# Weight loads on another queue and a sum two steps later, in a kernel of attention and two feed-forward layers

## The chip, the core and the metric

The kernel runs on one core of a Trainium2 chip. A core has five engines, each with its own instruction stream in a fixed order: TensorE (PE; its weight loads are shown as PEld), VectorE (DVE), ScalarE (ACT), GpSimd (POOL) and SyncE (SP), which here only asks for transfers. They wait for each other through semaphores. Transfers run on 16 DMA engines; an engine that asks for one spends time in its own stream on the request. The metric is device time in microseconds (us) of one execution, the median of several runs.

## The reference

Three stages follow each other; everything is float32 (weights of the two layers come as 64-bit floats).

```python
q_bits = (einsum('bhsd,dk->bhsk', q, proj) > 0)      # 6 bits each; k the same
mask = q_bucket[:, :, :, None] == k_bucket[:, :, None, :]
scores = where(mask, scale * q @ k.T, -1e9)
attn = exp(scores - max(scores)); attn = attn / (sum(attn) + 1e-9)
x = attn @ v                                         # 2 batches, 8 heads, 768 rows, 64 columns
x = ((1 / (1 + exp(-(x @ w_gate)))) * (x @ w_val)) @ w_out     # 1536 tokens, 512 -> 1536 -> 512
h = x @ w_in; y = (h * cos(h)) @ w_out2                        # 512 -> 2048 -> 512
```

## The kernel before

**The attention** goes over 96 steps g: 16 heads times 6 blocks of 128 query rows, with a tail of nine more steps. In each step a table of names (`ORDER`) says in which order parts of several blocks are issued; the order of instructions on each engine is the order in which the code issues them. For block g: `scores` (PE, two steps ahead), `rowmax` (DVE, L412), `expo` (ACT, L419: the exponential, one per step, so its starts mark the steps), `norm` (POOL, L454: scales a block's row by its sum, three steps later). Three blocks form a group u; a head has two. The three norms of a group are issued in three consecutive steps, all after `coef` of that group (DVE). Once they are done PE transposes the group, two column blocks a step (`ptrans`, L470), ACT and DVE split the result in a high and a low part (`phi` L475, `plo` L480), and PE multiplies with the values (`pv`, L490 and L491).

Every value tile holds a high and a low half, so the product `o` of a head has two halves of 64 partitions that must be added. `fin_act` (ACT, L499) copies `o` into `e`. At the end of a head pair, every 12 steps, it asks SP for two transfers that line up the halves, `ef<-e` (L507) and `e<-e` (L508). `fin_sum` (POOL, L513) then adds them, `fin_hi` (ACT, L529) and `fin_lo` (POOL, L533) split the sum into the layers' input `xy`. The call of step g puts these three into steps g + `SUM_AT`, g + `HIGH_AT` and g + `LOW_AT`, as the last piece (`PREP`) of the step. I call the step in which `fin_act` ends a pair the pair's end: 19, 31, 43, 55, 67, 79, 91 and 103.

Beside this run the inputs of later heads (`trans`: PE transposes, ACT evacuates into `xf` at L303, POOL splits into `x` at L304 and L307, SP distributes it at L348; `values`: POOL, L269 and L272, tile `vs`) and the first weights of the layers. `early_weights` (piece `W` of each step, behind the exponential) loads a weight block of 512 KB as 64-bit words into one of three `raw` tiles (`load_raw`, L133 and L139) at steps 14, 18 and 22, and from step 26 on converts one block in three steps, every ten steps, six in all (`convert_parts`: ACT `wp` L148, DVE L150, L154, L164). After the third part the tile is free and the next load is asked for.

**The layers** follow (`moe`): products on PE (L694, L756, L783), the rest of the weights loaded and converted on the way.

Of the kernel before, what the change touches and what calls it, by code (L numbers as in the profile page):

```python
# [18 lines left out]
P = 128  # L19
# [8 lines left out]
BITS_AT = (-10, -7)  # L28
VALUES_AT = (-3, -1)

SUM_AT, HIGH_AT, LOW_AT = 1, 5, 5
BIG = float(2.0**34)
CUT = float(2.0**30)
INV2PI = 1.0 / (2.0 * math.pi)
# [5 lines left out]
def lsh_attention_glu_moe_cos_moe(  # L40
# [13 lines left out]
    nc = tc.nc  # L54
# [16 lines left out]
    NEARLY = 6  # L71
# [9 lines left out]
    def constants():  # L81
        srow = xy[NC - 1].bitcast(F32)[0:1, 0, 0, 0 : 2 * D].rearrange("p (d two) -> p d two", two=2)
        make_identity(nc, ident)
        nc.vector.memset(pw.bitcast(F32), 0.0)
        nc.vector.memset(qscale[0:D], -SCALE)
        nc.vector.memset(qscale[D:P], 1.0)
        nc.vector.memset(halfpi, math.pi / 2)
        nc.vector.memset(quarter, 0.25)


        nc.vector.memset(srow, 0.0)
        k0, half = D // 2, BIG / 2
        for part, value, lo, hi in (
            (0, 1.0, 0, 3 * NB),
            (1, -1.0, 2 * NB, 3 * NB),
            (0, -BIG, k0, k0 + NB),
            (0, half, k0 + NB, k0 + 3 * NB),
            (1, -1.0, k0 + NB, k0 + 2 * NB),
        ):
            nc.vector.memset(srow[:, lo:hi, part : part + 1], value)  # L100
# [24 lines left out]

    raws = {}

    def load_raw(key):
        nm, f, _ = key
        rw = wraw.tile([P, 512], I64, tag="raw", name=f"raw_{nm}{f}")  # L130
        if nm in ("g", "v", "i"):
            src = {"g": w_gate, "v": w_val, "i": w_in2}[nm]
            nc.sync.dma_start(  # L133
                rw.rearrange("p (k c) -> p k c", k=KT),
                src[:, f * P : (f + 1) * P].rearrange("(k p) c -> p k c", p=P),
            )
        else:
            src = {"o": w_out1, "z": w_out2}[nm]
            nc.sync.dma_start(rw, src[f * P : (f + 1) * P, :])  # L139
        raws[key] = rw  # L140

    def convert_parts(key):
# [63 lines left out]
    def lead(key):  # L206
        nm, f, again = key
        if again:
            return 4, 2
        return {"g": (8, 4), "v": (7, 3), "i": (6, 3), "o": (5, 2), "z": (4, 3)}[nm]  # L210

    order = sorted(use, key=lambda kk: use[kk] - lead(kk)[0])
    done = 0
# [7 lines left out]

    loaded = 0

    def load_to(n):
        nonlocal loaded
        while loaded < min(n, len(order)):
            load_raw(order[loaded])
            loaded += 1


    def attention():
        nonlocal done
        parts = None
        with ExitStack() as st:
# [14 lines left out]
            def load(hd, nm, t0=0, t1=T, eng=nc.sync):  # L249
                b, h = divmod(hd, H)  # L250
                if nm == "v":
                    raw[hd, "v"] = nat.tile([P, 2, T * D], F32, tag="nv", name=f"nv{hd}", bufs=1)
                    nc.sync.dma_start(
                        raw[hd, "v"], v[b, h : h + 2].rearrange("h (p t) d -> p h (t d)", p=P)
                    )
                    return
                if hd not in raw:
                    raw[hd] = nat.tile([P, T, 2 * D], F32, tag="nqk", name=f"nqk{hd}")
                i = "qk".index(nm)
                eng.dma_start(  # L260
                    raw[hd][:, t0:t1, i * D : (i + 1) * D],
                    (q, k)[i][b, h].rearrange("(p t) d -> p t d", p=P)[:, t0:t1, :],
                )
# [274 lines left out]
            WL, WC = (14, 18, 22), 26  # L538
# [32 lines left out]
            def run_todo(step):  # L571
                for fn in todo.pop(step, []):
                    e = fn()
                    if e is not None:
                        late.append(e)

            with tc.manual_schedule(
                engines={
                    mybir.EngineType.PE,
                    mybir.EngineType.Activation,  # L580
                    mybir.EngineType.DVE,
                    mybir.EngineType.Pool,
                    mybir.EngineType.SP,
                }
            ):
                for t0 in (0, 3):
                    load(0, "q", t0, t0 + 3)
                    load(0, "k", t0, t0 + 3, eng=nc.scalar)
                constants()
                for g in range(2):  # L590
                    nc.sync.dma_start(pj[D * g : D * g + D, :], proj)
                nc.sync.dma_start(
                    bcode, xy[NC - 1].bitcast(F32)[0:1, 0, 0, 0 : 2 * D].rearrange("p (d two) -> p d two", two=2)
                )
                load(1, "q")
                load(1, "k")
                load(0, "v")
                load(2, "k")
                load(2, "q")
                bit_weights()  # L600
                evac = [trans(0, half, fast=True) for half in range(2)]
                for fn in evac:
                    fn()
                evac = [bits(0, half) for half in range(2)]
                evac += [trans(1, half, fast=True) for half in range(2)]
                for fn in evac:
                    fn()
                values(0)
                values(1)
                run_todo(-2)  # L610
                run_todo(-1)
                scores(0)
                scores(1)
                rowmax(0)
                late.extend(bits(1, half) for half in range(2))
                for g in range(NG + LAG + 2):
                    wa, wb = 2 * (g - LAG), 2 * (g - LAG) + 1
                    fin = (wb - 2) // T if 0 <= wb - 2 < NW and (wb - 2) % T == T - 1 else None

                    def finish_group():  # L620
                        fin_act(fin)
                        if fin % 4 == 3:
                            at(g + SUM_AT, lambda u=fin: fin_sum(u))
                            at(g + HIGH_AT, lambda u=fin: fin_hi(u))
                            at(g + LOW_AT, lambda u=fin: fin_lo(u))

                    def early_weights():
                        nonlocal done, parts
                        if g in WL:
                            load_to(1 + WL.index(g))  # L630
                        if done < NEARLY and g >= WC and (g - WC) % WSTEP == 0:
                            parts = convert_parts(order[done])
                        if parts is not None and next(parts, parts) is parts:
                            parts = None
                            done += 1
                            load_to(done + 3)

                    live_a, live_b, live_g = 0 <= wa < NW, 0 <= wb < NW, g < NG
                    third = 0 < g <= NG and g % 3 == 0
                    ops = {  # L640
                        "PVb": (0 <= wb - 2 < NW, lambda: pv(wb - 2)),
                        "FIN": (fin is not None, finish_group),
                        "Tb": (live_b, lambda: ptrans(wb)),
                        "LOa": (live_a, lambda: plo(wa)),
                        "EXP": (live_g, lambda: expo(g)),
                        "PVa": (live_a and fin is None, lambda: pv(wa)),
                        "MIN": (g + 1 < NG, lambda: rowmax(g + 1)),
                        "HIb": (live_b, lambda: phi(wb)),
                        "Ta": (0 <= wa + 2 < NW, lambda: ptrans(wa + 2)),
                        "COEF": (third, lambda: coef(g // 3 - 1)),  # L650
                        "LOb": (live_b, lambda: plo(wb)),
                        "NRM": (0 <= g - 3 < NG, lambda: norm(g - 3)),
                        "LATE": (True, run_late),
                        "W": (True, early_weights),
                        "S": (g + 2 < NG, lambda: scores(g + 2)),
                        "PVaF": (live_a and fin is not None, lambda: pv(wa)),
                        "PREP": (True, lambda: run_todo(g)),
                        "HIa": (0 <= wa + 2 < NW, lambda: phi(wa + 2)),
                    }
                    for name in ORDER if g >= LAG - 1 else FILL:  # L660
                        on, fn = ops[name]
                        if on:
                            fn()
                for step in sorted(todo):
                    run_todo(step)
# [209 lines left out]
```

## Time and profile before

| | us |
|---|---|
| median of 3 runs | 837.98 |
| lowest, highest | 836.65, 838.01 |
| the profiled execution: its time | 835.46 |
| the profiled execution: its span, first to last instruction | 833.7 |
| busy in the span: PE, DVE, ACT, POOL | 803.9, 601.4, 464.2, 327.1 |

The rows below come from the profiled execution. Times count from the start of its span; 1.76 us of its own time lie outside the span. Idle time of an engine is put down to the last releaser that the profile sees.

### The profile page before, as it was taken

What the parts mean: (1) busy time and instruction counts of PE and PEld (TensorE: products, weight loads), DVE (VectorE), ACT (ScalarE), POOL (GpSimd) and SP (SyncE); (2) the same over time, 40 slices, a digit from 0 to 9 for tenths busy, and PEclk for the clock granted to TensorE, in tenths of its full rate; (3) what the DMA queues carried; (4) which work ended last, traced back from release to release, by engine and by line L of the source; (5) the groups of instructions that cost most, each with busy time, mean ns of one, the idle gap of its engine ahead of it and who ended that gap; (6) DMA issues with size and microseconds to landing.
All of it is one profiled execution on the core that took longest, in us unless ns stands there. A gap on an engine that the chain in (4) does not pass through costs nothing.

```text
span 833.7 us, 11798 instructions
## 1 busy us (share of the span) xinstructions
PE 803.9 (96%) x3984; PEld 678.4 (81%) x3984; DVE 601.4 (72%) x996; ACT 464.2 (56%) x896; POOL 327.1 (39%) x315
## 2 busy tenths in 40 slices
PE   6998999999988999999999999999999999999998
PEld 4888788978877888888888888888788888868886
DVE  7998989989988444555554248787777777787773
ACT  5887788888877322233223234456666666664442
POOL 4858788787776211122112112230322222222221
PEclk9999999999999999999999999999999999999999
DMA  7775766576531223222232112341333323333222
GB/s 161 181 193 134 183 160 156 144 179 166 133 74 29 70 77 102 76 76 76 75 91 91 47 51 76 102 127 50 109 96 99 97 84 99 101 104 133 95 74 101
DMA packets 69068, 89.05 MB, mean 107 GB/s; under 512 B 29520, under 2 KB 52048, under 8 KB 69008
## 3 DMA queue, kind: packets, MB, share of 16 engines
q1 hardware_dynamic: 68208, 88.10, 37.7%
q8 instruction: 31, 0.51, 0.3%
q10 hardware_dynamic: 800, 0.20, 0.1%
q14 instruction: 29, 0.24, 0.1%
HBM read 59.77 MB, written 3.15 MB: 75 GB/s over the span
## 4 chain that ended last, share of the span: by engine, by line
PE 78%; POOL 5%; DMA 4%; issue 4%; ACT 4%; DVE 4%; SPq 1%; ACTq 0%; POOLq 0%; DVEq 0%
PE a L783 15%; PE ph L694 13%; PE pv L694 12%; PE a L756 12%; PE pg L694 12%; PE t L470 4%; POOL p L454 2%; PE s L401 2%; PE s L404 2%; PE o L491 2%; PE o L490 2%; DMA ef<-e 2%; ACT p L419 1%; DMA e<-e 1%; POOL ef L513 1%
## 5 line engine op out<-in xcount | busy, mean ns | idle before, releaser
L694 PE MATMUL ph<-xy,ih 128*128 128x512 f32 x384 | 118.2, 389 | 0.0
L480 DVE TENSOR_TENSOR pl<-t,ph 128x384 fp32r<-128x384 f32 x192 | 102.8, 549 | 20.8 <-ACT ph L475 18.7
L120 ACT CAST gh<-g 128x512 fp32r<-128x512 f32 x84 | 52.1, 620 | 112.4 <-PE a L783 44.8
L470 PE MATMUL t<-ident,p 128*128 128x128 f32 x576 | 99.6, 280 | 13.3 <-POOL p L454 10.0
L475 ACT CAST ph<-t 128x384 fp32r<-128x384 f32 x192 | 92.4, 484 | 31.4 <-PE t L470 26.1
L121 POOL TENSOR_TENSOR zl<-w_z,zh 128x512 fp32r<-128x512 f32 x32 | 41.9, 1310 | 169.8 <-ACT zh L120 169.8
L454 POOL TENSOR_SCALAR p<-p,r,d 128x768 f32<-128x768 f32 x96 | 96.3, 1014 | 3.3 <-PE o L491 3.3
L470 PEld LDWEIGHTS t<-ident,p 128*128 128x128 f32 x576 | 73.7, 143 | 28.6 <-POOL p L454 13.0
L720 DVE TENSOR_TENSOR g<-pv,sg 128x512 f32<-128x512 f32 x36 | 24.8, 689 | 98.6 <-PE pv L694 98.6
L412 DVE TENSOR_REDUCE mn<-s 128x1 f32<-128x768 f32 x96 | 91.1, 949 | 1.0 <-PE s L404 0.8
L419 ACT ACTIVATE p<-s,mn 128x768 f32<-128x768 f32 x96 | 87.8, 914 | 3.9 <-DVE mn L412 3.6
L694 PE MATMUL pg<-xy,gh 128*128 128x512 f32 x288 | 89.4, 390 | 0.0
L694 PE MATMUL pv<-xy,vh 128*128 128x512 f32 x288 | 88.7, 389 | 0.0
L718 ACT ACTIVATE sg<-pg 128x512 f32<-128x512 f32 x36 | 21.4, 593 | 114.0 <-PE pg L694 114.0
L694 PEld LDWEIGHTS ph<-xy,ih 128*128 128x128 f32 x384 | 72.1, 188 | 14.9
L121 DVE TENSOR_TENSOR gl<-g,gh 128x512 fp32r<-128x512 f32 x84 | 59.7, 713 | 32.8 <-ACT gh L120 30.6
L490 PE MATMUL o<-ph,vs 128*128 128x384 f32 x192 | 79.9, 416 | 0.3 <-ACT e L499 0.3
L783 PE MATMUL a<-zh,gh 128*128 128x512 f32 x192 | 75.0, 391 | 1.1 <-ACT gh L120 0.4
L783 PE MATMUL a<-zl,gh 128*128 128x512 f32 x192 | 75.0, 390 | 0.7 <-POOL zl L121 0.7
L783 PE MATMUL a<-zh,gl 128*128 128x512 f32 x192 | 74.8, 390 | 0.0
L694 PE MATMUL ph<-xy,il 128*128 128x512 f32 x192 | 74.7, 389 | 0.0
L401 PE MATMUL s<-k,q 96*128 96x384 f32 x192 | 69.9, 364 | 4.4 <-ACT p L419 3.0
(107 smaller groups left out, 1835.4 us busy)
## 6 DMA issues: line engine op xcount, KB each, us to landing
raw_z<-in_moe_w_out SPq DMA_DIRECT2D x32, 512.0 KB, 3.3
raw_o<-in_moe_w_out SPq DMA_DIRECT2D x24, 512.0 KB, 3.3
q<-x SPq DMA_DIRECT2D x45, 192.0 KB, 3.1
k<-x SPq DMA_DIRECT2D x45, 192.0 KB, 3.4
raw_i<-in_moe_w_in SPq DMA_DIRECT2D x16, 512.0 KB, 3.8
raw_g<-in_moe_w_gate SPq DMA_DIRECT2D x12, 512.0 KB, 3.6
raw_v<-in_moe_w_val SPq DMA_DIRECT2D x12, 512.0 KB, 3.8
nv<-in_v SPq DMA_DIRECT2D x8, 384.0 KB, 4.5
```

The costliest lines, as they stand in the source:

```text
L121: sub.tensor_tensor(out=dst_l, in0=src, in1=dst_h.bitcast(F32), op=ALU.subtract)
L401: nc.tensor.matmul(o, hh["q2"][0:96, t, :], hh["k2"][0:96, sl, :], start=True, stop=False)
L412: nc.vector.tensor_reduce(mn_t[u][:, i : i + 1], s_t[g], axis=AX.XY, op=ALU.min)
L419: nc.scalar.activation(pt, s_t.pop(g), AF.Exp, bias=mn_t[u][:, i : i + 1], scale=-1.0, accum_out=sm_t[u][:, i : i + 1],)
L454: nc.gpsimd.tensor_scalar(out=pt, in0=pt, scalar1=r[:, i : i + 1], scalar2=d[:, i : i + 1], op0=ALU.mult, op1=ALU.add,)
L470: nc.tensor.transpose(pt[:, i, :], pv_[:, j * P : (j + 1) * P], ident)
L475: nc.scalar.copy(ph, pt_t[w])
L480: nc.vector.tensor_tensor(out=pl, in0=pt_t.pop(w), in1=ph_t[w].bitcast(F32), op=ALU.subtract)
L490: nc.tensor.matmul(o_t[u], vs[:, j, :], ph_t.pop(w), start=(j == 0), stop=False)
L694: nc.tensor.matmul(ps, w[:, kt, :], xy[c][:, hl, kt, :], start=(n == 0), stop=(n == 11))
L756: nc.tensor.matmul(acc[c, e], w[:, e, :], m, start=(f == 0 and n == 0), stop=(f == F1 - 1 and n == 2),)
L783: nc.tensor.matmul(acc[c, t], m[:, ts], w, start=(f == 0 and n == 0), stop=(f == F2 - 1 and n == 2),)
```

## The change

The weight loads that `early_weights` asks for go on ACT's queue and no longer on SP's. The load that follows a conversion is asked for in the step after the conversion's third part, not in the same step. `fin_sum` is issued three steps after a pair's end, not one. Loads in the layers stay on SP.

```diff
-SUM_AT, HIGH_AT, LOW_AT = 1, 5, 5
+SUM_AT, HIGH_AT, LOW_AT = 3, 5, 5
...
-    def load_raw(key):
+    def load_raw(key, eng):
...
-            nc.sync.dma_start(
+            eng.dma_start(
...
-            nc.sync.dma_start(rw, src[f * P : (f + 1) * P, :])
+            eng.dma_start(rw, src[f * P : (f + 1) * P, :])
...
-    def load_to(n):
+    def load_to(n, eng=nc.sync):
         nonlocal loaded
         while loaded < min(n, len(order)):
-            load_raw(order[loaded])
+            load_raw(order[loaded], eng)
             loaded += 1
...
                         if g in WL:
-                            load_to(1 + WL.index(g))
+                            load_to(1 + WL.index(g), nc.scalar)
                         if done < NEARLY and g >= WC and (g - WC) % WSTEP == 0:
                             parts = convert_parts(order[done])
                         if parts is not None and next(parts, parts) is parts:
                             parts = None
                             done += 1
-                            load_to(done + 3)
+                        elif parts is None and 0 < done <= NEARLY:
+                            load_to(done + 3, nc.scalar)
```

The instructions of PE and DVE stand in the same order as before. On POOL seven of the eight sums move (the last has nothing left to pass); here is the first, of the pair that ends at step 19, before:

```order
L454 TENSOR_SCALAR p_779<-p_779,r_827,d_828 128x768
L513 TENSOR_TENSOR ef_641<-e_519,ef_641 128x768
L304 TENSOR_SCALAR x_5_807<-xf_964 128x384
L307 TENSOR_TENSOR x_5_808<-xf_964,x_5_807 128x384
L454 TENSOR_SCALAR p_835<-p_835,r_948,d_949 128x768
L269 TENSOR_SCALAR vs_986<-nv_863 128x6x64
L272 TENSOR_TENSOR vs_986<-nv_863,vs_986 128x6x64
L454 TENSOR_SCALAR p_875<-p_875,r_948,d_949 128x768
L454 TENSOR_SCALAR p_909<-p_909,r_948,d_949 128x768
```

and with the change:

```order
L454 TENSOR_SCALAR p_779<-p_779,r_827,d_828 128x768
L304 TENSOR_SCALAR x_5_807<-xf_963 128x384
L307 TENSOR_TENSOR x_5_808<-xf_963,x_5_807 128x384
L454 TENSOR_SCALAR p_835<-p_835,r_947,d_948 128x768
L269 TENSOR_SCALAR vs_985<-nv_863 128x6x64
L272 TENSOR_TENSOR vs_985<-nv_863,vs_985 128x6x64
L454 TENSOR_SCALAR p_875<-p_875,r_947,d_948 128x768
L513 TENSOR_TENSOR ef_641<-e_519,ef_641 128x768
L454 TENSOR_SCALAR p_909<-p_909,r_947,d_948 128x768
```

The sum stood ahead of the split of `x`, the values and all three norms of the next group; now it stands behind all of these but the group's third norm.

ACT's stream gains nine requests. This is the one of step 29, after the first conversion; `p` is the exponential of the step, `ph` the high part of a transposed block. Before:

```order
L419 ACTIVATE p_1287,sm_1167<-s_1233,mn_1166 128x768
L475 CAST ph_1296<-t_1279 128x384
L475 CAST ph_1306<-t_1289 128x384
L419 ACTIVATE p_1343,sm_1294<-s_1264,mn_1293 128x768
L303 ACTIVATE xf_1353<-pt_1321,qscale 128x384
```

and with the change:

```order
L419 ACTIVATE p_1285,sm_1167<-s_1233,mn_1166 128x768
L133 DMA raw_v_1294<-in_moe_w_val 128x4x128
L475 CAST ph_1296<-t_1277 128x384
L475 CAST ph_1306<-t_1287 128x384
L419 ACTIVATE p_1343,sm_1292<-s_1262,mn_1291 128x768
L303 ACTIVATE xf_1353<-pt_1321,qscale 128x384
```

The request stands between the exponential and the step's two high parts; in three of the nine steps the evacuation `xf` lies between the exponential and the request.

## Rows read from the trace of the kernel before

**Rows 1.** Windows: busy time per engine (instructions), granted TensorE clock, DMA share, GB/s.

```profile
25.00:60.00 35.00, 34.43 (x230) 31.63 (x229) 33.29 (x70) 29.92 (x68) 25.19 (x29) 1.00 0.76 189
60.00:75.00 15.00, 12.74 (x74) 11.31 (x73) 11.28 (x21) 10.80 (x25) 11.82 (x13) 0.89 0.71 164
...
72.00:74.00 2.00, 2.00 (x10) 1.81 (x8) 1.42 (x3) 1.98 (x6) 2.00 (x3) 0.50 1.05 284
...
300.00:570.00 270.00, 270.00 (x1193) 223.65 (x1192) 151.37 (x202) 92.31 (x164) 56.57 (x43) 1.00 0.26 82
```

**Rows 2.** Timeline of ACT, exponentials of steps 24, 27, 45, 48, 51, 54, 84, 87.

```profile
65.95 0.91 ACT L419 ACTIVATE p<-s,mn 128x768 f32<-128x768 f32 x1
...
77.33 0.91 ACT L419 ACTIVATE p<-s,mn 128x768 f32<-128x768 f32 x1
...
125.98 0.91 ACT L419 ACTIVATE p<-s,mn 128x768 f32<-128x768 f32 x1
...
133.63 0.91 ACT L419 ACTIVATE p<-s,mn 128x768 f32<-128x768 f32 x1
...
142.40 0.91 ACT L419 ACTIVATE p<-s,mn 128x768 f32<-128x768 f32 x1
...
149.80 0.91 ACT L419 ACTIVATE p<-s,mn 128x768 f32<-128x768 f32 x1
...
228.53 0.91 ACT L419 ACTIVATE p<-s,mn 128x768 f32<-128x768 f32 x1
...
238.99 0.91 ACT L419 ACTIVATE p<-s,mn 128x768 f32<-128x768 f32 x1
```

**Rows 3.** Timeline of POOL, first sum and what follows; the sixth sum.

```profile
62.93 1.83 POOL L513 TENSOR_TENSOR ef<-e,ef 128x768 f32<-128x768 f32 x1 [4.98 <-issue]
64.73 0.51 POOL L304 TENSOR_SCALAR x<-xf 128x384 fp32r<-128x384 f32 x1
...
66.33 0.99 POOL L454 TENSOR_SCALAR p<-p,r,d 128x768 f32<-128x768 f32 x1
67.28 0.52 POOL L269 TENSOR_SCALAR vs<-nv 128x384 fp32r<-128x384 f32 x1
...
68.86 1.95 POOL L454 TENSOR_SCALAR p<-p,r,d 128x768 f32<-128x768 f32 x2
...
225.63 1.85 POOL L513 TENSOR_TENSOR ef<-e,ef 128x768 f32<-128x768 f32 x1 [4.49 <-DMA e<-e]
```

**Rows 4.** Timeline of PE, transposes of a new group after sums one, three and six.

```profile
68.27 0.30 PE L470 MATMUL t<-ident,p 128*128 128x128 f32 x1
...
136.99 0.33 PE L470 MATMUL t<-ident,p 128*128 128x128 f32 x1 [0.58 <-POOL p L454]
...
230.22 0.27 PE L470 MATMUL t<-ident,p 128*128 128x128 f32 x1
```

**Rows 5.** Waits: engine, line, releaser, us in total, times, longest.

```profile
PE t L470 <- POOL p L454: 10.0, 11, 2.1
```

**Rows 6.** Timeline of ACT, evacuations xf, a conversion, the high part of a sum.

```profile
60.14 0.58 ACT L303 ACTIVATE xf<-pt,qscale 128x384 f32<-128x384 f32 x1 [0.60 <-PE pt L288]
...
130.12 0.67 ACT L148 ACTIVATE wp_g<-raw_g 128x512 f32<-128x512 f32 x1
...
137.73 0.93 ACT L529 CAST xy<-ef 128x512 fp32r<-128x512 f32 x2
...
222.73 0.58 ACT L303 ACTIVATE xf<-pt,qscale 128x384 f32<-128x384 f32 x1 [0.60 <-PE pt L288]
```

**Rows 7.** Source L513: shortest, median, longest of eight sums in ns.

```profile
L513 POOL TENSOR_TENSOR ef<-e,ef x8: 1829/1844/2509, 62.9 to 278.9; 128x768 f32<-128x768 f32 x8
```

**Rows 8.** Timeline of DVE beside the sum that starts at 159.97.

```profile
160.10 0.67 DVE L154 SCALAR_TENSOR_TENSOR wl_v<-wp_v,wl_v 128x512 int32<-128x512 int32 x1
```

**Rows 9.** Timelines of the queues: ACT's two requests, SP's longest in this stage.

```profile
0.73 1.06 ACTq L260 DMA_DIRECT2D nqk<-in_k  x2
...
149.41 1.49 SPq L260 DMA_DIRECT2D nqk<-in_k  x1
```

## The prediction, made before the changed kernel ran

> **What bounds the kernel now.** I read the windows first, to see which stage can give anything. In the layers PE has no gap: 270.00 of 270 us between 300 and 570 [rows 1]. Nothing in the change touches that stage, so what counts is when the attention ends, at about 275 us. In its undisturbed stretches PE is busy 34.43 of 35 us and DVE 33.29, ACT 29.92, so three engines are nearly full together; in the window 60 to 75 PE has 12.74 of 15 and all the others have dropped as well [rows 1]. Something holds them all there.
>
> Next the timeline of ACT, because its one exponential per step is a clock of the steps. Undisturbed, three steps take 149.80 − 142.40 = 7.40 us [rows 2]. The three steps 24 to 27 take 77.33 − 65.95 = 11.38, and steps 84 to 87 take 238.99 − 228.53 = 10.46 [rows 2]. I measured all 25 stretches of three steps between step 12 and step 87 in this way. Six are long, those that begin five steps after the end of a head pair (24, 36, 48, 60, 72, 84), with 11.38, 11.34, 8.77, 9.52, 8.87 and 10.46, together 60.34 us. Six undisturbed ones would be 44.40. The excess is **15.94 us**, and it is all that this change could return.
>
> Its origin is in POOL's timeline. The first sum (L513) starts at 62.93 after 4.98 us of idle POOL, waiting for the transfers that line up the halves; behind it stand x, the values and the three norms of the next group, of which the last two run as a pair from 68.86 [rows 3]. PE transposes the first of the three blocks at 68.27 and must wait for the other two [rows 4]; over the kernel it waits 10.0 us for norms in 11 places [rows 5]. The wait spreads to DVE and ACT, and in two of the six places the granted clock then falls to the lower of TensorE's levels, 1.2 GHz (0.50 between 72 and 74) [rows 1], right behind PE's wait.
>
> **The sum moved by two steps.** POOL reaches the first sum's old place at about 58 us and has to wait. Without the sum there, x starts when ACT's xf is done, 60.14 + 0.58, so at about 60.8 [rows 6]. From there the distances of the rows hold: 1.60 from x to the norm (64.73 to 66.33), 0.95 to the values, 1.58 to the second norm (67.28 to 68.86), 0.97 for it (half of 1.95) [rows 3]. That puts the sum at 65.9, three microseconds after it could start before. The sixth sum is the latest of its kind: it could start at 225.63 [rows 3], and its new place is 222.73 + 0.58 + 0.1 + 5.1 = 228.5 [rows 6]. So all six sums find their data there, with at least 2.9 us to spare, and POOL's wait is gone.
>
> What is late next is the group's third norm, since 1.84 us of sum [rows 7] now stand ahead of it. First pair: 65.9 + 1.84 + 0.99 = 68.7. PE would want this block a quarter of a microsecond behind the first, at 68.5 [rows 4], so it waits about 0.25. Sixth pair: 223.4 + 7.9 = 231.3 against 230.22 + 0.25 [rows 4], a wait of 0.86. The same sum for the four between gives 0 to 0.3. In total **1.7 us** of waiting stay.
>
> Two costs in the long stretches are not the sum's and stay too. First the high part of the sum: 0.93 us on ACT ahead of an exponential [rows 6]. In the stretch 48 to 51 (8.77, so 1.37 too long [rows 2]) PE waits only 0.58 for norms [rows 4]; the other 0.8 I put down to those casts. Taken five times, and 0.3 for the sixth, whose 3.06 are nearly all waits for norms (the longest, of 2.1 us [rows 5], is there), that is **4.3 us**. Second, conversions overlap the first two long stretches: an undisturbed stretch with one (45 to 48) takes 133.63 − 125.98 = 7.65, 0.25 more [rows 2], so **0.5**. Left over is what is removed: 15.94 − 1.7 − 4.3 − 0.5 = **9.4 us**. The seventh sum moves as well, but there POOL's norms wait for weight splits of the layers in any case; the eighth keeps its place. I count nothing for either.
>
> One rule speaks against the 1.84. The longest sum took 2.51 us [rows 7], and DVE's L154 started beside it, at 160.10 [rows 8]. The Trainium skill, SBUF — State Buffer, "Who interferes with whom", says that a DVE instruction with two SBUF inputs and a GpSimd instruction that reads SBUF exclude each other for a whole instruction; L154 is one, and this row agrees. By the rule, sums that land beside such an instruction in their new place would be the longer ones; by the median row they are not. It is the first rival below.
>
> **The requests on ACT.** Nine requests leave SP and enter ACT's stream. SP gains nothing that matters: behind them it stood waiting for POOL's x anyway. No conversion waits for these loads either, as each has at least 12 steps from its request, about 30 us. The raw tile has been free since DVE's L164 of the step before, so I see no wait at the request. The price is the request itself: two took 1.06 us at the start, 0.53 each [rows 9], so 4.8 us of ACT in all. How much reaches the path? The nearest row is a conversion's 0.67 us on ACT [rows 6], which together with its DVE parts lengthens a stretch by 0.25 [rows 2]. A request has no DVE part; I take 0.1 for each, **0.9 us**. What hides the rest is ACT's slack: it waits 0.60 for PE ahead of xf once in three steps [rows 6]. Bounds: nothing, if that slack takes all of it, and 4.8 if none; should a request last as long as SP's longest in this stage, 1.49 [rows 9], 13.4.
>
> **The sum**: 835.46 − 9.4 + 0.9 = 826.96 for the profiled execution. That one lies 2.5 us below the median of the runs shown, so against the median I expect 837.98 − 8.5 = **829.5 us**.
>
> **The rivals.** (1) The sum delays the third norm more: at 2.51 us for all six sums, 0.67 × 6 = 4.0 us come back, 833.5. For it: one of eight sums shows this length. Against: the median is 1.84. (2) The requests are not hidden: 4.8 instead of 0.9, so 833.4. For it: outside the steps with xf, ACT runs without a gap. Against: the conversions cost so little. (3) The other side, slower: each request holds ACT for 1.49 us and nothing hides it. Then 13.4 are lost against 9.4 won: 842.0. It decides from 1.04 us a request on. Against it: the only requests of ACT took 0.53. (4) The casts' 4.3 us were an echo of the stall and go too, and the third norms are not late either: 15 gained, 823. For it: stretches after a long step run faster for a while, so ACT has some slack to catch up. Against: the casts occupy ACT wherever they stand. (5) The change does not do what it says: the sum waits in its new place too, because the weight loads now run beside the copies and not in line with them. The Trainium skill, DMA: Bandwidth & Descriptors, "Queues, rings and completion order", has each DMA engine take turns between the queues; no row here shows two loaded queues. In rows: the copies would have to land over 2.9 us later to bring back any wait, and 838 is reached only if all six do so by about 6 us. Few loads are asked for near a copy (steps 18, 29 and 79), so I find it unlikely.
>
> **How the numbers follow.** Forecast 0.60, rival 1 0.10, rival 2 0.12, rival 3 0.05, rival 4 0.09, rival 5 0.04. The range 824.5 to 834.5 holds the forecast and rivals 1 and 2 and leaves out 3, 4 and 5. A change of 0.2% (1.7 us) is about what a measurement of this kernel can tell from none. Forecast, 1, 2 and 4 are faster by more: 0.91; rival 5 is the same: 0.04; rival 3 slower: 0.05.
>
> **What would show it.** In the changed kernel's profile no sum should have idle time before it that ends with a transfer, except the last; the long stretches should fall from 60.3 to about 51 us in all; PE should wait about 2 us for norms, not 10.0; the granted clock should stay at the higher level (2.4 GHz) until the attention's tail. Nine requests of about 0.5 us should stand in ACT's queue, the exponential behind each hardly later. I am wrong if PE still waits for norms behind the sum (third norm), or if the steps 14, 18, 22, 29, 39 and so on become visibly longer (requests).

## The result, and the profile after

| | before, timed beside it | after |
|---|---|---|
| median, us | 837.32 | 827.16 |
| lowest, highest | 834.59, 838.01 | 825.95, 830.04 |
| the profiled execution: time, span | 835.46, 833.7 | 826.00, 824.2 |

The ratio is 0.989, 95% interval 0.985 to 0.993: the kernel is 10.2 us faster, by the interval between 6 and 12 us. The forecast was 8.5 us faster and 829.5; the time lies in the range.

The waits of the changed kernel come first (engine, what it waits for, us in total, times, longest):

```profile
POOL ef L513 <- DMA e<-e: 9.8, 1, 9.8
...
PE t L470 <- POOL p L454: 2.7, 4, 0.8
```

PE's wait for norms fell from 10.0 us in 11 places [rows 5] to 2.7 in 4, and of the eight sums only the last, which kept its place, still waits for its transfer. The timeline of POOL in the changed kernel shows the first sum in its new place, and the sixth:

```profile
65.11 1.00 POOL L454 TENSOR_SCALAR p<-p,r,d 128x768 f32<-128x768 f32 x1
66.06 1.85 POOL L513 TENSOR_TENSOR ef<-e,ef 128x768 f32<-128x768 f32 x1
67.87 0.99 POOL L454 TENSOR_SCALAR p<-p,r,d 128x768 f32<-128x768 f32 x1
...
222.71 1.84 POOL L513 TENSOR_TENSOR ef<-e,ef 128x768 f32<-128x768 f32 x1
```

No idle time stands before them, where there were 4.98 and 4.49 us [rows 3] (the first of these is put down to issue there, and not to a transfer). POOL reaches the sum at 66.06; 65.9 was forecast. The group's third norm is now behind it, at 67.87. PE does not wait for it at this pair, but it does at the third, fourth and sixth, as the timeline of PE in the changed kernel shows; the last two rows belong to the tail of the attention:

```profile
132.31 0.33 PE L470 MATMUL t<-ident,p 128*128 128x128 f32 x1 [0.33 <-POOL p L454]
...
164.15 0.33 PE L470 MATMUL t<-ident,p 128*128 128x128 f32 x1 [0.83 <-POOL p L454]
...
225.57 0.33 PE L470 MATMUL t<-ident,p 128*128 128x128 f32 x1 [0.73 <-POOL p L454]
...
256.94 0.44 PE L491 MATMUL o<-pl,vs 128*128 128x384 f32 x1 [1.14 <-DVE pl L480]
...
258.46 0.33 PE L470 MATMUL t<-ident,p 128*128 128x128 f32 x1 [0.80 <-POOL p L454]
```

The exponentials give the stretches of three steps again, in us:

| stretch from step | 24 | 36 | 48 | 60 | 72 | 84 | sum | step 12 to 95 | step 95 to the end |
|---|---|---|---|---|---|---|---|---|---|
| before | 11.38 | 11.34 | 8.77 | 9.52 | 8.85 | 10.46 | 60.3 | 219.3 | 578.1 |
| after | 8.54 | 9.09 | 8.91 | 8.78 | 8.20 | 8.21 | 51.7 | 211.2 | 576.5 |

The six long stretches lost 8.6 us. One that was undisturbed, 39 to 42, went from 7.40 to 8.15, and the one from step 27 fell from 7.91 to 7.67. That makes 8.1 us between steps 12 and 95. The rest of the profiled executions' 9.5, some 1.5 us, lies behind step 95. Windows of the changed kernel (busy time per engine with its instructions, granted clock, DMA share, GB/s):

```profile
60.00:75.00 15.00, 14.59 (x95) 12.76 (x93) 14.38 (x25) 12.91 (x30) 13.76 (x15) 1.00 0.81 172
...
258.00:260.00 2.00, 1.54 (x11) 1.43 (x12) 1.14 (x4) 0.75 (x2) 1.65 (x2) 1.00 0.00 0
260.00:262.00 2.00, 2.00 (x16) 1.70 (x14) 1.95 (x4) 1.35 (x4) 0.00 (x0) 1.00 0.00 0
```

and of the kernel before at the same place of the tail, which there comes 8 us later:

```profile
266.00:268.00 2.00, 1.58 (x6) 1.40 (x7) 1.00 (x3) 0.48 (x1) 1.60 (x2) 0.60 0.00 0
268.00:270.00 2.00, 2.00 (x10) 1.86 (x9) 1.15 (x2) 1.04 (x3) 0.00 (x0) 0.55 0.00 0
```

Between 60 and 75 PE now works 14.59 us and not 12.74 [rows 1], at the higher level of the clock (2.4 GHz); in windows of 4 us of the changed kernel the granted clock is 1.00 in every one from 16 to 300 us. In the tail the work is the same, but in the profiled execution of before the clock fell to the lower level for a while (0.60 and 0.55), and in that of after it did not. Those 1.5 us are no work of the moved instructions: kernel e2 below, which gains nothing, has 576.5 there as well. They belong to this pair of profiled executions; whether they are in the medians, the runs don't show.

A request stands in ACT's timeline of the changed kernel (step 29, behind the first conversion), between an exponential and a high part:

```profile
77.52 0.91 ACT L419 ACTIVATE p<-s,mn 128x768 f32<-128x768 f32 x1
...
78.59 0.48 ACT L475 CAST ph<-t 128x384 fp32r<-128x384 f32 x1
...
79.89 0.90 ACT L419 ACTIVATE p<-s,mn 128x768 f32<-128x768 f32 x1
80.48 0.37 ACTq L133 DMA_DIRECT2D raw_v<-in_moe_w_val  x1
...
80.96 0.48 ACT L475 CAST ph<-t 128x384 fp32r<-128x384 f32 x1
```

The request runs in ACT's queue while the exponential is still computing (79.89 + 0.90 = 80.79). From an exponential's start to the next high part it is 1.07 us with the request (79.89 to 80.96) and without (77.52 to 78.59). All nine took 0.35 to 0.41 us. All began while another instruction of ACT was at work: four beside an exponential, three beside an evacuation `xf`, two beside a high part. The stretches from step 12, 15, 18 and 21, in which three of them fall, are 7.40 long as before.

### The profile page after: what moved, and what is told of

Same layout as the page of the kernel before. It is cut to its first block, busy times and chain, and to the rows that moved or that the text cites. A ratio compares the mean times of both kernels' runs of the same rounds, so it can differ in the third digit from the quotient of the medians.

```text
span 824.2 us, 11783 instructions
## 1 busy us (share of the span) xinstructions
PE 801.0 (97%) x3984; PEld 673.7 (82%) x3984; DVE 604.7 (73%) x996; ACT 464.1 (56%) x896; POOL 325.8 (40%) x315
## 4 chain that ended last, share of the span: by engine, by line
PE 82%; DVE 9%; ACT 4%; issue 2%; POOL 1%; DMA 0%; ACTq 0%; DVEq 0%; POOLq 0%
PE a L784 15%; PE ph L695 14%; PE pv L695 12%; PE a L757 12%; PE pg L695 12%; PE t L470 5%; PE s L401 3%; PE s L404 3%; PE o L491 3%; PE o L490 2%; DVE mn L412 2%; PE pb L362 2%; DVE pl L480 2%; PE pt L288 1%; ACT p L419 1%
## 5 line engine op out<-in xcount | busy, mean ns | idle before, releaser
L470 PE MATMUL t<-ident,p 128*128 128x128 f32 x576 | 96.9, 275 | 6.2 <-POOL p L454 2.7
L412 DVE TENSOR_REDUCE mn<-s 128x1 f32<-128x768 f32 x96 | 91.0, 948 | 0.6 <-PE s L404 0.4
L470 PEld LDWEIGHTS t<-ident,p 128*128 128x128 f32 x576 | 71.3, 140 | 22.3 <-issue 9.7
```

Of the source, the lines that this page charges most:

```text
L412: nc.vector.tensor_reduce(mn_t[u][:, i : i + 1], s_t[g], axis=AX.XY, op=ALU.min)
L470: nc.tensor.transpose(pt[:, i, :], pv_[:, j * P : (j + 1) * P], ident)
```

## The experiments

Seven kernels ran, four timed beside one set of runs of the kernel before (median 837.13), three beside another (837.4).

**e1 and e2: the two halves of the change alone.** e1 is the kernel before with the sum at three steps:

```diff
-SUM_AT, HIGH_AT, LOW_AT = 1, 5, 5
+SUM_AT, HIGH_AT, LOW_AT = 3, 5, 5
```

> The kernel before with the sum two steps later and nothing else; loads stay on SyncE's queue, in their old step. Theory (the sum is the whole gain, the requests on ScalarE cost and give nothing): the six long stretches of three steps fall from 60.3 us to 51 to 52.5 in all, PE waits for norms about 3 us, and the time is 9 to 10 us below before, that is ratio 0.988 to 0.990. Rival (moving the loads off SyncE gives part of the gain, because copies of the sum no longer queue behind a load): less than 7 us gained, ratio above 0.992.

e2 is the changed kernel with the sum put back to one step:

```diff
-SUM_AT, HIGH_AT, LOW_AT = 3, 5, 5
+SUM_AT, HIGH_AT, LOW_AT = 1, 5, 5
```

> The changed kernel with the sum back at one step after a pair's end: only the loads are on ScalarE's queue, one step later. Theory: GpSimd again idles 3 to 5 us before each of the first six sums, the six long stretches stay at 60 us, and the time is that of before within 0.2%. Rival A (each request costs ScalarE 0.1 us on the path, as predicted): 0.9 us slower, ratio 1.001. Rival B (the loads' move gives part of the gain): over 2 us faster, ratio below 0.998.

e1 measured 828.16 us, ratio 0.9899 (0.9885 to 0.9913), long stretches 51.8. e2 measured 836.62, ratio 0.9990 (0.9973 to 1.0007, that is from 2.3 us faster to 0.6 slower), long stretches 61.0; its waits for norms are back:

```profile
PE t L470 <- POOL p L454: 10.3, 12, 2.1
```

So the sum brings the whole gain, and moving the loads neither wins nor costs what can be measured; the 0.9 us of rival A lie outside the interval. In the profiled executions e1 takes 0.9 us longer between steps 12 and 95 than the changed kernel, and e2 1.4 longer than the kernel before. In each, the two stretches from step 75 are 1.0 us longer, and that is not the loads' doing (last section). The Trainium skill, DMA: Bandwidth & Descriptors, "Issuing engines are not separate DMA queues", says that asking from another engine saves only that engine's time on the request, since all transfers share the 16 DMA engines. e2 agrees: SP's time on the requests was worth nothing here.

**e3: the sum at two steps.** There the sum stands ahead of the group's second and third norms, and no longer beside the coefficients of the next group on DVE (L435 to L445). In the changed kernel these short operations had become long. DVE's timeline of the changed kernel in the stretch from step 36:

```profile
97.55 1.20 DVE L435 TENSOR_SCALAR r<-sm 128x3 f32<-128x3 f32 x1
...
98.99 0.70 DVE L445 SCALAR_TENSOR_TENSOR r<-mn,r 128x3 f32<-128x3 f32 x1
...
103.26 0.94 DVE L154 SCALAR_TENSOR_TENSOR wl_v<-wp_v,wl_v 128x512 int32<-128x512 int32 x1
...
105.92 1.34 DVE L164 SCALAR_TENSOR_TENSOR w_v<-raw_v,wl_v 128x512 int32<-128x512 int32 x1
```

POOL's timeline of the changed kernel beside it:

```profile
96.88 1.84 POOL L513 TENSOR_TENSOR ef<-e,ef 128x768 f32<-128x768 f32 x1
98.70 0.98 POOL L454 TENSOR_SCALAR p<-p,r,d 128x768 f32<-128x768 f32 x1
...
104.78 1.94 POOL L454 TENSOR_SCALAR p<-p,r,d 128x768 f32<-128x768 f32 x2
```

L435 ends at 98.75, just after the sum (98.72); L445 ends at 99.69, just after the norm (99.68). I took this for what is left in the long stretches.

```diff
-SUM_AT, HIGH_AT, LOW_AT = 3, 5, 5
+SUM_AT, HIGH_AT, LOW_AT = 2, 5, 5
```

> The changed kernel with the sum two steps after a pair's end, so ahead of the group's second norm and not behind it; the copies have landed by then and the third norm is as late as with three. Theory (what is left of the long stretches is mostly VectorE's reciprocal of the row sums, L435 and L445, held up by GpSimd's running sum: 1.19 and 0.70 us where 0.15 and 0.16 are usual): the sum now runs a microsecond earlier and ends just as L435 starts, L435 falls below 0.5 us beside it, the six long stretches fall from 51.7 to about 47 and the time by 3 to 5 us against the change. Rival 1 (the casts of the high part on ScalarE, as predicted): 51.7 stays, the same time as the change within 1 us. Rival 2 (the late third norm): also unchanged.

Measured: 826.00, ratio 0.9872 (0.9857 to 0.9888). DVE's timeline of e3 in the same stretch:

```profile
100.14 0.23 DVE L435 TENSOR_SCALAR r<-sm 128x3 f32<-128x3 f32 x1
...
100.61 0.70 DVE L445 SCALAR_TENSOR_TENSOR r<-mn,r 128x3 f32<-128x3 f32 x1
...
104.90 0.67 DVE L154 SCALAR_TENSOR_TENSOR wl_v<-wp_v,wl_v 128x512 int32<-128x512 int32 x1
...
107.38 0.68 DVE L164 SCALAR_TENSOR_TENSOR w_v<-raw_v,wl_v 128x512 int32<-128x512 int32 x1
```

and POOL's:

```profile
107.40 2.49 POOL L454 TENSOR_SCALAR p<-p,r,d 128x768 f32<-128x768 f32 x2
```

L435 is short again in five of the six groups (0.17 to 0.23 us; 0.64 in the fourth), while L445 still stands beside the next norm and keeps its 0.70 (0.55 in the third). Only two stretches gain: 36 to 39 (9.09 to 8.19) and 39 to 42 (8.15 to 7.41), 1.6 us together. There a conversion follows the sum on DVE: in the changed kernel, late from the sum, DVE came to L154 and L164 while POOL was at work, and they took 0.94 and 1.34. In e3 they begin just ahead of POOL's instruction and take 0.67, and it is the pair of norms that grows (2.49, and 1.94 in the changed kernel). In the other five long stretches L435 fell as well, and they changed by at most 0.03. So the theory holds in one place, and falls for the rest: 50.8 was measured where 47 was expected. The medians differ by 1.2 us, less than the changed kernel's own runs do (825.95 to 830.04), so the 1.6 rest on the profiled executions.

**e4: the sum at four steps**, behind all three norms, so that none waits for it:

```diff
-SUM_AT, HIGH_AT, LOW_AT = 3, 5, 5
+SUM_AT, HIGH_AT, LOW_AT = 4, 5, 5
```

> The changed kernel with the sum four steps after a pair's end, so behind all three norms of the group. Rival 2 (the late third norm is what is left): PE's waits for norms at the six places vanish, the long stretches fall from 51.7 to 50 or less and the time by about 2 us against the change. Theory (VectorE held up by the sum): the sum now starts a microsecond later and meets L445, which should take about 1.5 us instead of 0.70, while L435 gets shorter; the long stretches gain under 1 us. Rival 1 (casts): the high part now has to wait for the sum on ScalarE, or stays at 0.8 us a pair; no gain.

Measured: 826.62, ratio 0.9885 (0.9869 to 0.9901). PE waits for a norm once, 0.8 us in the tail, but the long stretches are 51.6 and not 51.7. In the stretch from step 48 the first step fell from 4.63 to 4.39, and the second rose from 2.33 to 2.97. DVE's timeline of e4 in that first step:

```profile
130.38 1.83 DVE L435 TENSOR_SCALAR r<-sm 128x3 f32<-128x3 f32 x1
...
132.61 0.94 DVE L412 TENSOR_REDUCE mn<-s 128x1 f32<-128x768 f32 x1
```

POOL's and ACT's timelines of e4 beside it:

```profile
130.37 1.82 POOL L513 TENSOR_TENSOR ef<-e,ef 128x768 f32<-128x768 f32 x1
```

```profile
133.59 0.90 ACT L419 ACTIVATE p<-s,mn 128x768 f32<-128x768 f32 x1 [0.21 <-DVE mn L412]
...
135.21 0.48 ACT L475 CAST ph<-t 128x384 fp32r<-128x384 f32 x1 [0.63 <-DVE pl L480]
```

The sum now starts with L435, which takes the sum's whole 1.8 us; the row's maximum behind it (L412) comes late, and the exponential waits for that. In the second step DVE is still behind, and ACT waits 0.63 us for its low part. In the first, second, fourth and sixth group it is L445 that is held, as expected (1.53 to 1.55 us), while L435 falls to 0.35 (0.77 in the fourth): together as long as in the changed kernel. The stretches from 60 and 84, where PE had waited 0.83 and 0.73 for a norm, gained only 0.23 and 0.24; those from 48 and 72 lost 0.41 and 0.25. So the third norm's wait can be taken away, but the six stretches together gain next to nothing by it (0.1 us).

**e5: the casts twice.** The high part of the sum (L529) is issued twice:

```diff
-                for h, _, x in pieces(u):
-                    nc.scalar.copy(h, x)
+                for _ in range(2):
+                    for h, _, x in pieces(u):
+                        nc.scalar.copy(h, x)
```

> The changed kernel with the two casts of the high part (L529) issued twice, the second time into the same place with the same values. Theory (what is left of the six long stretches, 51.7 against 44.4 us undisturbed, is mostly these casts on ScalarE ahead of an exponential): each long stretch becomes about 0.9 us longer, the six together 56 to 58 us, the time 4 to 6 us above the change. Rival (the late third norm or VectorE's held-up small operations set these stretches, and the casts lie beside that wait): under 2 us in all.

Measured: 830.20, ratio 0.9920 (0.9898 to 0.9943), 3.0 above the changed kernel; long stretches 55.4, so 3.7 more. That is a little less than was expected (56 to 58, and 4 to 6 above), and more than the rival's 2. ACT's timeline in the changed kernel, first pair:

```profile
66.13 0.91 ACT L419 ACTIVATE p<-s,mn 128x768 f32<-128x768 f32 x1
...
69.67 0.93 ACT L529 CAST xy<-ef 128x512 fp32r<-128x512 f32 x2
70.49 0.90 ACT L419 ACTIVATE p<-s,mn 128x768 f32<-128x768 f32 x1
```

and in e5:

```profile
66.00 0.91 ACT L419 ACTIVATE p<-s,mn 128x768 f32<-128x768 f32 x1
...
69.54 1.75 ACT L530 CAST xy<-ef 128x512 fp32r<-128x512 f32 x4
71.19 0.90 ACT L419 ACTIVATE p<-s,mn 128x768 f32<-128x768 f32 x1
```

The step takes 5.19 and not 4.36: the added casts (1.75 − 0.93 = 0.82) reach the next exponential whole. The stretches from 24, 60, 72 and 84 grow by 0.81 to 0.83 each, that from 48 by 0.39, that from 36, where DVE is the bound, not at all. Between steps 12 and 95 e5 takes 4.8 us longer; 1.0 of that lies in the stretches from step 75, as in e1 and e2, and behind step 95 it is 1.1 shorter, for which the runs show no cause. The casts are a cost of their own, not an echo of the stall: the stall is gone in both kernels. What a second pair of casts adds need not be what the first one costs; e7 tries the other side.

**e6: the request in the step of the conversion**, on ACT's queue but not a step later:

```diff
-                        elif parts is None and 0 < done <= NEARLY:
                             load_to(done + 3, nc.scalar)
```

> The changed kernel with the weight load still on ScalarE's queue, but asked for in the same step as the conversion's third part, as it was on SyncE's. Theory (the request is free only where the raw tile is free already): ScalarE's queue now waits at the request for VectorE's L164 of the same step, 1 to 2 us at each of six requests, with the step's high parts and the next exponential behind it; the stretches with a request become 0.5 to 1.5 us longer, the time 3 to 8 us above the change. Rival (ScalarE's slack hides it): the same as the change within 1 us.

Measured: 841.52, ratio 1.0048 (1.0025 to 1.0071): 4 us slower than the kernel before, 14 slower than the changed one, where 3 to 8 were expected. ACT's timeline in e6, where the change has the rows at 79.89 to 80.96:

```profile
78.74 0.91 ACT L419 ACTIVATE p<-s,mn 128x768 f32<-128x768 f32 x1
...
81.70 0.37 ACTq L133 DMA_DIRECT2D raw_v<-in_moe_w_val  x1
82.17 0.48 ACT L475 CAST ph<-t 128x384 fp32r<-128x384 f32 x1 [2.44 <-DVE w_g L164]
```

The request must wait until DVE has read the raw tile, and all of ACT stands behind it for 2.44 us. Step 12 to 95 takes 226.8 us instead of 211.2. About 1.0 of these 15.6 is what e1, e2 and e5 show in the stretches from step 75 as well (last section), so six such requests cost some 2.4 us each. "One step later" is what makes the request free.

**e7: the casts in a gap.** ACT waits 0.60 us for PE ahead of xf once in three steps [rows 6]. Here the sum goes to two steps, as in e3, and the casts of seven of the eight pairs leave the step's last piece for the place ahead of xf:

```diff
-SUM_AT, HIGH_AT, LOW_AT = 3, 5, 5
+SUM_AT, HIGH_AT, LOW_AT = 2, 5, 5
...
-                            at(g + HIGH_AT, lambda u=fin: fin_hi(u))
+                            if fin < NW // T - 1:
+                                at(g + 4, lambda u=fin: late.insert(0, lambda: fin_hi(u)))
+                            else:
+                                at(g + HIGH_AT, lambda u=fin: fin_hi(u))
```

> The changed kernel with the sum two steps after a pair's end and the casts of the high part moved ahead of the evacuation xf in the fifth step after it, where ScalarE idles 0.6 us for PE once in three steps; the low part stays. Theory (the casts cost because they stand right ahead of an exponential): most of the 0.8 us a pair goes, the six long stretches fall from 50.8 (sum at two steps) to 47 to 48.5 us, the time by 2 to 4 us against the sum at two steps, to 822 to 824. Rival (the late third norm sets these stretches): within 1 us of the sum at two steps.

Measured: 822.48, ratio 0.9829 (0.9803 to 0.9855), the fastest of all, 4.7 below the changed kernel and 3.5 below e3. ACT's timeline in e7, first pair:

```profile
67.38 0.91 ACT L419 ACTIVATE p<-s,mn 128x768 f32<-128x768 f32 x1
...
68.26 0.92 ACT L529 CAST xy<-ef 128x512 fp32r<-128x512 f32 x2
69.08 0.59 ACT L303 ACTIVATE xf<-pt,qscale 128x384 f32<-128x384 f32 x1
...
70.91 0.91 ACT L419 ACTIVATE p<-s,mn 128x768 f32<-128x768 f32 x1
```

No wait stands before xf now, and the step takes 3.53 us against 4.36 in the changed kernel. The long stretches are 48.3 (50.8 in e3). Not all of the 2.5 us remains: the stretch from 27 grew from 7.65 to 8.43, and step 12 to 95 is 208.06 against 209.43, so 1.4 us are left. Of the 3.5 us to e3, the profiled executions put 1.4 between those steps, 0.8 behind them, and 1.3 ahead of step 12. That start is no part of the edit: from the first exponential to that of step 12 the nine profiled executions took 23.6 to 26.3 us, whatever the kernel. It is 25.0 or more in the four (e1, e3, e6, e7) whose granted clock fell to the lower level between 22 and 30 us (0.50 to 0.59 in a window of 2 us), and at most 24.1 in the others. What made the 0.8 behind step 95, the runs don't show. So the long stretches and the time came out as expected, but of the 3.5 us the profiled executions show only 1.4 as the casts' new place.

## Why the prediction was right, point by point

**The mechanism** was the one forecast: the sums waited for their transfers, the norms behind them came late, and PE, DVE and ACT stood. With the sum two steps later that wait is gone (e1 has all of the gain, e2 none). The removed part was put at 9.4 us; it measured 8.6 in the six stretches, less 0.75 given back in the stretch from step 39, so 7.9. One reading was off and changed nothing: in the window 60 to 75 not all other engines had dropped, POOL was busier (11.82 of 15 us against 25.19 of 35 [rows 1]).

**What is late next.** The third norm was forecast to make PE wait 1.7 us. The three rows of PE show 0.33 + 0.83 + 0.73 = 1.9 before the tail. The sum is near, its parts less so: the fourth pair was put at 0.3 at most, and the first at 0.25, where PE does not wait at all. Whether these 1.9 reach the end in full stays open: e4 took the wait away, but put a hold-up on DVE in its place. Rival 1, long sums, falls with the source view of the changed kernel:

```profile
L513 POOL TENSOR_TENSOR ef<-e,ef x8: 1837/1842/2316, 66.1 to 269.4; 128x768 f32<-128x768 f32 x8
```

Of the six sums only the third is long (2.32 us); L154 stands beside it, from 128.91.

**The casts** were put at 4.3 us. Doubled (e5), they add 0.82 in four of the places, 0.39 in one and nothing in the one where DVE is full: 3.7. Moved away (e7), they give back 2.5 in the long stretches. So they are a cost that stays, as forecast, and rival 4 (an echo) falls; their size is 2.5 to 3.7 us rather than 4.3. What the prediction said against rival 4, that the casts occupy ACT wherever they stand, is too strong: in e7 they fill a gap.

**What was left out** is the hold-up on DVE. The rule on DVE and POOL was weighed only as a price on the sum, which it did not raise (median 1.84 as before). It came out on the other side: POOL began first and DVE waited. The Trainium skill, SBUF — State Buffer, "Who interferes with whom", has this too: the ports that DVE and GpSimd share are an exclusive lock, and the order of issue decides which of the two is blocked. The rows of L154 and L164, with two inputs in SBUF, agree: behind POOL's instruction they took 0.94 and 1.34 us, ahead of it 0.67. Starts that lie some 0.1 us apart don't tell the order, though: in the kernel before, the sum at 159.97 grew to 2.51 although L154 began at 160.10. e3 priced the part of the hold-up that it removed at 1.6 us, about what the removed part was too large by. Of the 7.3 us still left in the long stretches (51.7 − 44.4) and the 0.75 behind them, the casts' 2.5 to 3.7 and these 1.6 have a cause that a run showed; how the other 2.8 to 4.0 divide between third norms, conversions and the rest of DVE's hold-up, the runs don't separate.

**The requests** were the mis-sized term with the other sign: 0.9 us were taken; e2 came out 0.5 us faster, and 0.6 slower at most by its interval. The prediction read 0.53 each from the two requests at the start and counted them against ACT's work. They took 0.35 to 0.41 and ran beside other instructions of ACT. Rivals 2 and 3 fall with that. That the raw tile is free one step later was right, and e6 shows the price had it not been: some 15 us.

**Rival 5**, late copies, falls with two rows of the changed kernel's DMA view (KB each, median us from issue to landing):

```profile
raw_v<-in_moe_w_val ACTq DMA_DIRECT2D x3, 512.0 KB, 5.7
...
e<-e SPq DMA_DIRECT2D x8, 192.0 KB, 4.6
```

The copies still land after 4.6 us (4.3 before) beside loads on the other queue.

**The sum of the terms** for the profiled executions: −7.9 for the removed waits less what came back, 0 for the requests and −1.5 for the clock in the tail give −9.4; the spans differ by 9.5. The forecast of 8.5 was near in part by luck: the removed part was 1.5 too large, and the requests' 0.9 and the clock's 1.5 more than made up for it. That holds for these two executions; the medians differ by 10.2, with an interval of 6 to 12, and what of that the clock made, the runs don't show. That the clock keeps its higher level through the stretches was forecast, and the windows show it; what it did in the tail was not.

## What to carry to other kernels

Before moving an instruction that waits for a transfer, find out on its own engine what stands behind it: here an instruction of 1.84 us, whose data were always there two steps later, had cost some 8 to 10 us. A request for a transfer on a computing engine is free if what it waits for is done when the engine gets there, and costs the whole wait if not; one step decided between nothing measurable and some 15 us. What a stall leaves over should be tried piece by piece: of two waits that looked alike, taking one away returned 1.6 us (e3) and the other nothing (e4). Compare single profiles stretch by stretch and not by their spans: at the start, in the steps from 75 and in the tail they differ by 1 to 2.7 us without any help from the edit.

## What the hardware showed that was not expected

- Operations of 128x3 on DVE, 0.15 us by themselves, took up to 1.6 us beside POOL (1.8 in e4). In the source view of the changed kernel

```profile
L435 DVE TENSOR_SCALAR r<-sm x32: 146/342/1612, 17.5 to 250.2; 128x3 f32<-128x3 f32 x32
```

  the longest is 1612 ns and the median 342. L435 has one tensor from SBUF and scalars, and was held to the sum's end, too.
- The granted clock did not follow from the wait alone. In the tail PE waits alike in both kernels, 1.14 and 0.80 us in the changed one, and the level fell in the one profiled execution and not in the other. What decides it, the runs don't show.
- Which of DVE and POOL comes first seems to be a matter of chance in one place, and is worth 1.0 us there. After step 75 a conversion's L150 and the second of three norms on POOL begin at about the same time. DVE's rows of the changed kernel and of e1:

```profile
204.86 0.50 DVE L150 TENSOR_SCALAR wl_o<-raw_o 128x512 int32<-128x512 int32 x1
```

```profile
206.15 1.28 DVE L150 TENSOR_SCALAR wl_o<-raw_o 128x512 int32<-128x512 int32 x1
```

  In both L150 begins 4.76 us after the exponential of step 75, and POOL's three norms at 3.80. In the changed kernel the norms take 3.21 us together and L150 is short; in e1 they take 3.09, L150 is held, and so is L154 behind it (1.26 and not 0.77). The stretches from 75 and 78 then take 16.25 us and not 15.27. e1, e2, e5 and e6 went the second way, the kernel before, the changed one, e3 and e4 the first; in e7 L150 comes later. Each was profiled once, so how often a kernel goes which way is not shown.
